# A fused attention and two-expert kernel on one core: attention output normalised in PSUM, low halves on either engine, a planner that keeps VectorE and GpSimd apart, and another order of tasks

## The chip, the cores and the metric

The kernel runs on one core of one Trainium2 chip. The metric is the device time of one execution in microseconds, the median of three runs. TensorE is the matrix engine (PE in the rows), VectorE is DVE, ScalarE is ACT, GpSimd is POOL, and SyncE (SP) issues the transfers.

## The reference

Attention with a bias that depends on the positions, then two expert layers on its output. Shapes: 4 batches, 8 heads, 576 positions, 64 elements a head; 2304 tokens of 512 elements; 2048 hidden elements.

```python
rel = (pos[:, None] - pos[None, :])
x = (np.log1p(np.abs(rel)) / np.log1p(np.maximum(pos[:, None], 1.0)))[..., None]
bias = np.maximum(x @ w1 + b1, 0.0) @ w2
scores = scale * np.matmul(q, k.transpose(0, 1, 3, 2)) + bias.transpose(2, 0, 1)[None]
attn = np.exp(scores - np.max(scores, axis=-1, keepdims=True))
attn = attn / (np.sum(attn, axis=-1, keepdims=True) + 1e-09)
x = np.matmul(attn, v)                       # to (2304, 512)
h = x @ w_in1; r = np.maximum(h, 0.0)
x = (s * (r * r) + b) @ w_out1               # first expert layer
h = x @ w_in2
out = (h - np.tanh(h)) @ w_out2              # second expert layer
```

## The kernel before

Every matmul operand is split into two half-precision parts, a high half (the value rounded) and a low half (what the rounding left), and products of halves are summed. So most values pass through a cast and a subtraction on their way.

**Attention.** The work is 144 units, each one pair of heads or half-rows by up to 128 query rows, and 36 groups of four units. A unit passes through these tasks: `qk` (12 matmuls on TensorE into `sp`, line 1003); `ttr` (VectorE, line 1035: adds the bias and finds the row's extreme) and a small addition to it on VectorE (line 1039); `ex` (the exponential with the row sum, ScalarE, line 1045); `hi` (the cast to `hl`, ScalarE line 1057 or VectorE line 1055); `lo` (the subtraction in two pieces of 64 and 512 columns, GpSimd, line 1064); `tr` (a transposing transfer, line 1070, `et` from `hl`); `pv` (14 matmuls into `xp`, lines 1083 and 1089). After the four units of a group, `x_tasks` normalises: VectorE adds a constant to the row sums (line 1127), inverts them (1128), multiplies the accumulator `xp` by them into an SBUF buffer `xf` (1129), casts that to `xh` (1143) and subtracts (1144); ScalarE squares `xf` for a norm (1147); a transfer transposes `xh` into `xt`.

**First expert layer.** Nine blocks of 256 tokens, tags f0 to f8. A block is 192 hidden-layer matmuls (`ph`, line 1499), passed on by eight rounds of ReLU (1512) and square (1517) on ScalarE, a cast (VectorE, 1522) and a subtraction (GpSimd, 1526) into `hr`, and 192 output-layer matmuls (`po`, line 1568), evacuated by VectorE (1582) or ScalarE (1587). The `po` tile is one bank of PSUM, whose two halves are used in turn. Lines 1194, 1197 and 1200 are three VectorE steps that convert a weight from 64-bit numbers; 585 and 580 split values into halves; 1775 sums weights; 1842, 2009 and 2018 are float32 sums of the second layer.

**Second expert layer.** Products of 24 matmuls (lines 1964 and 2092) on sums of quarter matrices; its weights are converted and split during the end of the first layer.

**What sets the order.** All of this is a list of tasks with priorities, and a planner in the kernel's file, `Schedule.forward`, plays them through on paper: each task has a cost per engine it may run on, corrected by a table `COST` (transfers by `XFER`), a priority corrected by a table `SHIFT`, and for some an engine fixed by `ENGINE` or `ONLY`. Rings of a given number of places (`ring`) hold back a task until a buffer is free in the plan. Tasks are emitted in the planned order, and every engine then works through its own queue in that order. When VectorE and GpSimd overlap in the plan, the cost of both grows by fractions called `SHARE` and `SHARE_POOL`. `AHEAD` is how far transfers may be issued ahead.

## Time and profile before

| quantity | us |
|---|---|
| median of three runs | 1077.86 |
| lowest, highest | 1072.72, 1078.9 |
| the profiled execution | 1072.9 |
| its span, first to last instruction | 1071.1 |

The mean granted clock of TensorE was 0.951. Busy time over the span: TensorE 962.1 us (90%), VectorE 898.9 (84%), ScalarE 664.7 (62%), GpSimd 350.7 (33%). These are averages over stretches that differ, so the rows below are cut by time: attention and the preparation of the first layer's weights to 171 us, attention together with the first layer to 560 us (the last score matmuls end at 559 us), the rest of the first layer to 741 us, and the second layer to the end.

### The profile page before, as it was taken

The numbers are of one execution on the slowest core, as the hardware profiler recorded it, in microseconds if no ns is written. First come the engines' busy times: TensorE is split into PE (matmuls) and PEld (weight loads), VectorE is DVE, ScalarE is ACT, GpSimd is POOL, SyncE is SP. The second block draws the span as 40 slices with busy tenths as digits, with TensorE's granted clock in tenths as the row PEclk, the third lists the DMA queues.
The fourth block names the chain that finished last, engine by engine and source line by source line (L and its number), as shares of the span: only waits on it lengthen the run. The fifth ranks groups of instructions, "written<-read, shape, count | busy, mean of one in ns | idle before, by whom it ended". The sixth has DMA issues, their size and how long they took to land.

```text
span 1071.1 us, 32375 instructions
## 1 busy us (share of the span) xinstructions
PE 962.1 (90%) x13370; PEld 820.5 (77%) x13370; DVE 898.9 (84%) x1914; ACT 664.7 (62%) x1279; POOL 350.7 (33%) x371
## 2 busy tenths in 40 slices
PE   5565658999998899999999898987999999999998
PEld 2222236778787688787888787877999999999998
DVE  6899899767668777786773989889999999999876
ACT  6788879868766576777753575656645543344433
POOL 6034355646456376585762342300000000000000
PEclk9667669999999999999999999999999999999999
DMA  9969987999999999989996705310101100100001
GB/s 340 360 153 250 296 230 149 208 211 255 244 181 234 201 171 199 206 172 194 173 171 167 300 10 173 105 36 16 32 23 41 42 22 31 32 22 22 21 2 41
DMA packets 261444, 153.66 MB, mean 143 GB/s; under 512 B 197680, under 2 KB 229552, under 8 KB 261296
## 3 DMA queue, kind: packets, MB, share of 16 engines
q1 hardware_dynamic: 261296, 151.59, 58.8%
q8 instruction: 104, 1.70, 0.7%
q14 instruction: 44, 0.36, 0.1%
HBM read 84.03 MB, written 20.33 MB: 97 GB/s over the span
## 4 chain that ended last, share of the span: by engine, by line
PE 55%; DVE 21%; DMA 12%; ACT 4%; issue 4%; POOL 3%; SPq 1%; DVEq 0%; ACTq 0%; POOLq 0%
PE acc L2092 13%; PE ph L1499 9%; PE pa L1964 8%; PE po L1568 8%; DMA et<-hl 8%; PE pb L1964 6%; PE sp L1003 3%; DVE w1big L585 3%; DVE sp L1035 2%; PE po L2092 2%; PE xp L1083 2%; POOL hr L692 1%; ACT e L1045 1%; DMA w1big<-in_wout 1%; DMA bi<-btd 1%
## 5 line engine op out<-in xcount | busy, mean ns | idle before, releaser
L1064 POOL TENSOR_TENSOR hl<-e,hl 128x64 f16<-128x64 f32 (+1 forms) x288 | 231.9, 828 | 221.0 <-ACT hl L1057 93.6
L1568 PE MATMUL po<-hr,w1big 128*128 128x256 f16 x1728 | 205.8, 275 | 13.2 <-ACT x L1587 8.6
L1568 PEld LDWEIGHTS <-w1big 128*128 128x128 f16 x1728 | 166.7, 99 | 39.2 <-issue 18.8
L1499 PEld LDWEIGHTS <-w1big 128*128 128x128 f16 x1728 | 165.2, 98 | 26.7 <-issue 8.0
L1964 PEld LDWEIGHTS <-w2big 128*128 128x128 f16 x3024 | 174.1, 98 | 4.2 <-issue 4.2
L2092 PEld LDWEIGHTS <-w1big 128*128 128x128 f16 x3024 | 172.8, 98 | 2.1 <-issue 2.1
L1045 ACT ACTIVATE e<-sp,mx 128x576 f32<-128x576 f32 x144 | 105.7, 734 | 53.7 <-DVE mx L1039 39.2
L1526 POOL TENSOR_TENSOR hr<-r,hr 128x512 f16<-128x512 f32 x72 | 100.4, 1396 | 115.8 <-DVE hr L1522 104.6
L1035 DVE CUSTOM_DVE_ANT_0 sp<-sp,bi 128x576 f32<-128x576 f32 x144 | 109.6, 761 | 31.9 <-PE sp L1003 26.5
L1499 PE MATMUL ph<-xt_own,w1big 128*128 128x256 f16 x960 | 112.5, 273 | 1.0 <-ACT r L1512 0.6
L1003 PE MATMUL sp<-ks,qs 64*128 64x288 f16 (+1 forms) x960 | 82.8, 298 | 13.9 <-ACT e L1045 11.3
L1083 PEld LDWEIGHTS <-et 128*128 128x128 f16 (+1 forms) x1440 | 54.9, 103 | 49.8 <-DMA et<-hl 26.6
L1499 PE MATMUL ph<-w1big 128*128 128x256 f16 x768 | 89.7, 275 | 1.6 <-ACT r L1512 1.2
L1083 PE MATMUL xp<-vp,et 128*128 128x64 f16 (+1 forms) x1440 | 65.5, 198 | 23.5 <-DMA et<-hl 17.8
L1057 ACT ACTIVATE hl<-e 128x576 f16<-128x576 f32 x100 | 67.5, 680 | 24.4 <-DMA et<-hl 21.1
L2092 PE MATMUL acc<-hr,w1big 128*128 128x128 f16 x1296 | 80.2, 219 | 1.8 <-DVE hr L585 1.2
L1003 PEld LDWEIGHTS <-qs 64*128 64x128 f16 (+1 forms) x960 | 46.3, 99 | 43.0 <-issue 32.8
L2092 PE MATMUL acc<-w2big,w1big 128*128 128x128 f16 x1296 | 79.1, 219 | 0.0
L1964 PE MATMUL pa<-w1big,w2big 128*128 128x128 f16 x960 | 61.2, 221 | 4.0 <-ACT w1big L1983 4.0
L1512 ACT ACTIVATE r<-ph 128x512 f32<-128x512 f32 x72 | 42.6, 592 | 31.0 <-PE ph L1499 22.4
L1522 DVE CAST hr<-r 128x512 f16<-128x512 f32 x72 | 42.2, 588 | 17.6 <-ACT r L1517 16.0
L1517 ACT ACTIVATE r<-r,sq 128x512 f32<-128x512 f32 x72 | 51.8, 720 | 1.5
(225 smaller groups left out, 1686.1 us busy)
## 6 DMA issues: line engine op xcount, KB each, us to landing
bi<-btd SPq DMA_DIRECT2D x64, 288.0 KB, 4.1
w1big<-in_wout SPq DMA_DIRECT2D x12, 1024.0 KB, 5.8
btd<-et SPq DMA_DIRECT2D x36, 295.5 KB, 4.4
w1big<-in_win SPq DMA_DIRECT2D x8, 1024.0 KB, 8.0
w2big<-in_win SPq DMA_DIRECT2D x8, 1024.0 KB, 12.8
x2d<-x SPq DMA_DIRECT2D x36, 128.0 KB, 2.2
w1big<-x2d SPq DMA_DIRECT2D x36, 128.0 KB, 2.4
outT<-xt_own SPq DMA_DIRECT2D x18, 256.0 KB, 2.2
```

Of the source, the lines that this page charges most:

```text
L1003: nc.tensor.matmul(out=out, lhsT=qs.tile[64 * h:64 * h + 64, sq, p * r:p * r + r], rhs=ks.tile[64 * h:64 * h + 64, sk, half * HS:(half + 1 ...
L1035: nc.vector.tensor_tensor_reduce(out=st, in0=st, in1=bi.tile.rearrange("p (a b) -> p a b", a=2), scale=-1.0 / KAP, scalar=3.0e38, op0=ALU. ...
L1045: nc.scalar.activation(out=put(e, row_tile("e")).rearrange("p (a b) -> p a b", a=2), in_=sp.tile[:, :, 0:HS], func=AF.Exp, scale=-1.0, bia ...
L1057: nc.scalar.activation(out=h[:, 0:S], in_=e.tile, func=AF.Copy)
L1064: (nc.gpsimd if eng == POOL else nc.vector).tensor_tensor(out=hl.tile[:, o:o + m], in0=e.tile[:, c:c + m], in1=hl.tile[:, c:c + m], op=ALU ...
L1083: nc.tensor.matmul(out=xp[r0:r0 + r, o:o + 64], lhsT=et.tile[:, n, r0:r0 + r], rhs=vp.tile[:, 0, n % 5, 64 * h:64 * h + 64], start=n == 0, ...
L1499: nc.tensor.matmul(out=ph.tile[:, fi, :], lhsT=win_ap(1, sw, m, f), rhs=xa(sx, m), start=m == 0 and j == 0, stop=m == KM - 1 and j == 2,)
L1517: nc.scalar.activation(out=r.tile, in_=r.tile, func=AF.Square, scale=sq[:, fp // 4:fp // 4 + 1])
L1526: (nc.gpsimd if e == POOL else nc.vector).tensor_tensor(out=rh[:, :, 1, :], in0=r.tile, in1=rh[:, :, 0, :], op=ALU.subtract)
L1568: nc.tensor.matmul(out=po.tile[:, :NB1], lhsT=wout_ap(1, sw, f, c), rhs=rhl[f // 8][:, f % 8, sr, :], start=f == 0 and j == 0, stop=f == K ...
L1964: nc.tensor.matmul(out=bank.tile[:, f * HT:(f + 1) * HT], lhsT=w[:, sw, m, f * 128:(f + 1) * 128], rhs=xs[:, sx, m], start=p in (1, 2, 5) ...
L2092: nc.tensor.matmul(out=bank.tile[:, o + c * HT:o + (c + 1) * HT], lhsT=w[:, sw, f, c * 128:(c + 1) * 128], rhs=g[:, sx, f], start=new and ...
```

## The change

- `x_tasks`: the buffer `xf` goes. `xp` becomes one tile of one bank, two halves used in turn, with a ring of 2. Scaling works in place in PSUM; cast (VectorE or ScalarE), subtraction (VectorE) and square (ScalarE) read PSUM; the constant and the inversion become tasks of their own, the constant on VectorE or GpSimd.
- The ring of `po` has 2 places in place of 1.
- The small addition behind `ttr`, both pieces of `lo` and the first layer's subtraction may run on VectorE or GpSimd; the first layer's cast on VectorE or ScalarE.
- The planner no longer stretches overlapping work: a VectorE task that uses the shared port (its `share` above 0) starts in the plan only when GpSimd's task is over, less 0.14 us, and the other way round. All tables are new, `AHEAD` is 8.71 for 5.97, a hold of SP's queue behind a late transfer is added.
- A block's hidden-layer matmuls are no longer chained behind the output-layer matmuls of the block before (`last = list(t_in1)`).

In the built program that gives these counts:

| task | before | after |
|---|---|---|
| first layer's subtraction | GpSimd 72 | GpSimd 34, VectorE 38 |
| first layer's cast | VectorE 72 | VectorE 12, ScalarE 60 |
| pieces of `lo` | GpSimd 288 | GpSimd 185, VectorE 103 |
| `hi` of a unit | VectorE 44, ScalarE 100 | VectorE 71, ScalarE 73 |
| addition behind `ttr` | VectorE 144 | VectorE 87, GpSimd 57 |
| cast of a group's output | VectorE 36 | VectorE 16, ScalarE 20 |
| `ph` and `po` matmuls ahead of unit 24's scores | 72, 0 | 12, 0 |
| `ph` and `po` matmuls ahead of unit 36's scores | 192, 188 | 192, 176 |
| `ph` and `po` matmuls ahead of the last scores | 1152, 1172 | 1248, 1184 |

Matmuls into `xp` that wait for VectorE or ScalarE on the same bank: 33 before, all for line 1129; 47 after, for accesses to the other half of the bank (27 line 1201, 8 line 1198, 5 line 1184, 4 line 1194, 3 line 1192). Matmuls into `po` that wait for an evacuation of the other half: 26 before, 27 after; 15 evacuations on ScalarE after the change also wait for matmuls into the other half.

```diff
@@ tables
-AHEAD = 5.97
+AHEAD = 8.71
-ONLY = {"I.fn": "dve", "I.sub": "dve", "J.fn": "dve", "J.c22": "dve", "I.add": "dve", "X.xsum": "dve", "P.wsum": "dve", "u.lo": "pool", "f.lo": "pool"}
+ONLY = {"I.fn": "dve", "I.sub": "dve", "J.fn": "dve", "J.c22": "dve", "I.add": "dve", "X.xsum": "dve", "P.wsum": "dve"}
 ENGINE = {
...
+    "f3.hi": "dve", "u0.mx_add": "dve", "f1.lo": "pool", "u2.mx_add": "dve", "u6.mx_add": "dve", "f8.lo": "dve",
+    "u12.mx_add": "dve", "f8.hi": "act", "f1.out": "act", "u16.lo_a": "pool", "u1.lo_a": "pool", "x6.eps":
...
@@ class Schedule, forward
-    SHARE, SHARE_POOL, SHARE_MAX = 0.65, 0.18, 2.1
+    BACK, BACK_MIN, BACK_HOLD = 0.5, 1.6, 1.1
+    LEAD, LONG = 0.14, 1.6
+    SHARE = 1.0
+                    if eng == "dve" and t.share > 0.0:
+                        at = max(at, port["pool"] - self.LEAD)
+                    elif eng == "pool" and t.opts[eng] < self.LONG:
+                        at = max(at, port["dve"] - self.LEAD)
-                if eng == "dve" and t.share > 0.0:
-                    rest = port["pool"] - at
-                    if rest > 0.0:
-                        cost = min(cost + t.share * rest, cost * self.SHARE_MAX)
-                        late("pool", self.SHARE_POOL * min(rest, cost))
-                    port["dve"], user["dve"] = at + cost, t
...
+                if eng == "pool" and cost < self.LONG or eng == "dve" and t.share > 0.0:
+                    port[eng] = at + cost
@@ rings
-("x", 1), ("h", 2), ("o", 1), ("r", 2), ("xt", 4), ("x2", 2), ("xf", 2), ("xh", 2), ("sum", 4),
+("x", 2), ("h", 2), ("o", 2), ("r", 2), ("xt", 4), ("x2", 2), ("xh", 2), ("sum", 4),
+    xp_all = ps_x.tile([128, 2, 256], F32, name="xp")
@@ units
-        t_lo = sc.add({POOL: 1.5, DVE: 0.7}, lo, [t_hi], d + 4, [], [e, hl])
+        t_lo = [
+            sc.add({POOL: 0.31, DVE: 0.15}, lo_a, [t_hi], d + 4, [], [e, hl]),
+            sc.add({POOL: 1.16, DVE: 0.69}, lo_b, [t_hi], d + 4, [], [e, hl]),
+        ]
-                put(xp_i, ps_x.tile([128, 512], F32, tag="xp", name="xp"))
+                put(xp_i, xp_all[:, xp_n(), :])
@@ x_tasks
+            x = xp_of[n].tile.rearrange("p (h d) -> p h d", d=64)
             nc.vector.tensor_tensor(
-                out=put(xf, x_p.tile([128, 256], F32, tag="xf", name="xf", bufs=2)).rearrange(
...
+                out=x, in0=x, in1=sum_of[n].tile.unsqueeze(2).to_broadcast([128, NP, 64]), op=ALU.mult,
...
+            if eng == DVE:
+                nc.vector.tensor_copy(out=xh.tile[:, 0:256], in_=xp_of[n].tile)
+            else:
+                nc.scalar.activation(out=xh.tile[:, 0:256], in_=xp_of[n].tile, func=AF.Copy)
...
+            nc.vector.tensor_tensor(out=xh.tile[:, 256:512], in0=xp_of[n].tile, in1=xh.tile[:, 0:256], op=ALU.subtract)
...
-                out=xf.tile, in_=xf.tile, func=AF.Square, accum_out=nrm[:, n:n + 1]
+                out=xp_of[n].tile, in_=xp_of[n].tile, func=AF.Square, accum_out=nrm[:, n:n + 1]
@@ first expert layer
-        last = t_poq.get(n - 1, [])[-1:]
+        last = list(t_in1)
-            def hi(_, rh=rh, r=r):
-                nc.vector.tensor_copy(out=rh[:, :, 0, :], in_=r.tile)
+            def hi(e, rh=rh, r=r):
+                if e == DVE:
+                    nc.vector.tensor_copy(out=rh[:, :, 0, :], in_=r.tile)
+                else:
+                    nc.scalar.activation(out=rh[:, :, 0, :], in_=r.tile, func=AF.Copy)
```

VectorE behind the last score tile, before: casts of the first layer (line 1522, `hr` from `r`) and the three conversion steps of the second layer's weights (`w2big`).

```order
L1522 CAST hr<-r 128x2x256 x4
L1194 TENSOR_SCALAR w2big<-w2big 128x1024
L1197 SCALAR_TENSOR_TENSOR w2big<-w2big 128x1024
L1522 CAST hr<-r 128x2x256
L1200 SCALAR_TENSOR_TENSOR w2big<-w2big 128x1024
```

The same place after: the subtraction (line 1584, which reads `r` and the high half in `hr`) stands where the cast stood.

```order
L1584 TENSOR_TENSOR hr<-r,hr 128x2x256 x3
L1248 TENSOR_SCALAR w2big<-w2big 128x1024
L1251 SCALAR_TENSOR_TENSOR w2big<-w2big 128x1024
L1584 TENSOR_TENSOR hr<-r,hr 128x2x256
L1254 SCALAR_TENSOR_TENSOR w2big<-w2big 128x1024
```

In each order 24 such instructions of the first layer stand behind the last score tile on VectorE: 24 casts before, 24 subtractions after.

ScalarE at that place, before: pairs of ReLU (line 1512, from `ph`) and square (1517).

```order
L1512 ACTIVATE r<-ph 128x512
L1517 ACTIVATE r<-r,sq_8369 128x512
L1512 ACTIVATE r<-ph 128x512
L1517 ACTIVATE r<-r,sq_8369 128x512
L1723 ACTIVATE junk,ss_w_137<-w2big 128x512 x2
```

After: the cast (line 1580) is the third of each round.

```order
L1567 ACTIVATE r<-ph 128x512
L1572 ACTIVATE r<-r,sq_8455 128x512
L1580 ACTIVATE hr<-r 128x2x256
L1567 ACTIVATE r<-ph 128x512
L1572 ACTIVATE r<-r,sq_8455 128x512
L1580 ACTIVATE hr<-r 128x2x256
L1781 ACTIVATE junk,ss_w_138<-w2big 128x512 x2
```

So 24 casts came to ScalarE's queue here, each between a square and the next ReLU.

TensorE at the first matmuls of the last group's attention output, before (in brackets the semaphore that the instruction waits for): score matmuls, then `xp`, which waits for VectorE's scaling of the group before.

```order
L1003 LDWEIGHTS qs
L1003 MATMUL sp<-ks,qs 128x288
L1083 LDWEIGHTS et [waits DMAHW4_49]
L1083 MATMUL xp<-vp,et 128x64 [waits DVE_49]
L1083 LDWEIGHTS et
L1083 MATMUL xp<-vp,et 128x64
```

After: output-layer matmuls, then `xp` (line 1131), which waits for ScalarE's square of the group before.

```order
L1626 LDWEIGHTS w1big
L1626 MATMUL po<-hr,w1big 128x256
L1131 LDWEIGHTS et [waits DMAHW6_49]
L1131 MATMUL xp<-vp,et 128x64 [waits Activation_49]
L1131 LDWEIGHTS et
L1131 MATMUL xp<-vp,et 128x64
```

The group before lies in the other half of the bank; the wait moved from VectorE's first step to ScalarE's last one.

## Rows read from the trace of the kernel before

**Rows 1.** Busy time by stretch: us, then busy and instructions per engine, granted clock, DMA share.

```profile
...
30.00:171.00 141.00, 88.25 (x755) 42.84 (x751) 133.50 (x259) 115.79 (x225) 47.14 (x45) 0.71 0.90 248
171.00:217.00 46.00, 42.23 (x630) 30.68 (x627) 39.86 (x89) 40.42 (x85) 31.79 (x34) 1.00 0.85 173
217.00:560.00 343.00, 328.55 (x4385) 272.18 (x4382) 252.22 (x685) 238.32 (x532) 207.82 (x254) 0.99 1.01 202
560.00:600.00 40.00, 39.02 (x470) 34.23 (x469) 19.92 (x41) 17.14 (x34) 14.03 (x11) 1.00 0.77 235
600.00:741.00 141.00, 122.41 (x1177) 107.50 (x1175) 129.37 (x194) 85.83 (x152) 29.72 (x17) 0.96 0.26 88
741.00:1040.00 299.00, 298.66 (x5339) 298.54 (x5337) 283.49 (x577) 139.10 (x208) 0.00 (x0) 1.00 0.09 27
...
```

**Rows 2.** Waits from 217 to 560 us: engine, line, releaser: total us, times, longest.

```profile
...
PEld L1083 <- DMA et<-hl: 9.8, 15, 1.6
...
PE xp L1083 <- DMA et<-hl: 5.9, 10, 1.0
...
PE sp L1003 <- ACT e L1045: 2.5, 3, 1.4
...
PE po L1568 <- ACT x L1587: 2.1, 3, 1.0
...
```

**Rows 3.** Timeline from 589 us: start, us, engine, line, operation.

```profile
...
588.75 7.37 PE L1499 MATMUL ph<-w1big 128*128 128x256 f16 x66
...
590.21 0.41 DVE L1522 CAST hr<-r 128x512 f16<-128x512 f32 x1
...
590.76 2.01 POOL L1526 TENSOR_TENSOR hr<-r,hr 128x512 f16<-128x512 f32 x1 [1.56 <-DVE hr L1522]
590.98 0.60 ACT L1512 ACTIVATE r<-ph 128x512 f32<-128x512 f32 x1 [1.27 <-PE ph L1499]
...
591.68 1.64 DVE L1194 TENSOR_SCALAR w2big<-w2big 128x1024 uint32<-128x1024 uint32 x1
...
```

**Rows 4.** VectorE groups by form, 560 to 741 us: busy us, mean ns, idle before.

```profile
...
L1522 DVE CAST hr<-r 128x512 f16<-128x512 f32 x24 | 13.7, 570 | 8.5 <-ACT r L1517 7.4 <-issue 1.1
L1197 DVE SCALAR_TENSOR_TENSOR w2big<-w2big 128x1024 uint32<-128x1024 uint32 x8 | 11.4, 1439 | 0.1
...
L1194 DVE TENSOR_SCALAR w2big<-w2big 128x1024 uint32<-128x1024 uint32 x8 | 8.2, 1042 | 0.0
L1197 DVE SCALAR_TENSOR_TENSOR w2big<-w1big,w2big 128x1024 uint32<-128x1024 uint32 x4 | 4.9, 1215 | 0.0
...
L1842 DVE TENSOR_TENSOR w1big<-w1big 128x256 f32<-128x256 f32 x8 | 4.1, 536 | 0.0
L1200 DVE SCALAR_TENSOR_TENSOR w2big<-xt_own,w2big 128x512 uint32<-128x512 uint32 x4 | 3.7, 920 | 0.0
...
L1194 DVE TENSOR_SCALAR w2big<-w1big 128x1024 uint32<-128x1024 uint32 x4 | 2.9, 726 | 0.9 <-DMA w1big<-in_wout 0.9
...
L1200 DVE SCALAR_TENSOR_TENSOR w2big<-w2big 128x512 uint32<-128x512 uint32 x4 | 2.7, 678 | 0.0
...
```

**Rows 5.** GpSimd groups by form, the whole span.

```profile
...
L1064 POOL TENSOR_TENSOR hl<-e,hl 128x512 f16<-128x512 f32 x144 | 178.2, 1238 | 0.0
...
```

**Rows 6.** VectorE groups by form, 741 to 1040 us, where GpSimd is idle.

```profile
...
L2009 DVE TENSOR_TENSOR w1big<-w1big 128x512 f32<-128x512 f32 x30 | 20.5, 684 | 4.2 <-ACT w1big L2000 4.1
...
L1842 DVE TENSOR_TENSOR w1big<-w1big 128x256 f32<-128x256 f32 x28 | 11.1, 414 | 0.0
...
```

**Rows 7.** VectorE groups by form, 217 to 560 us.

```profile
...
L1129 DVE TENSOR_TENSOR xf<-xp,sum 128x256 f32<-128x256 f32 x26 | 11.0, 425 | 8.7 <-PE xp L1089 6.9
...
```

**Rows 8.** Waits from 560 to 741 us.

```profile
...
PE po L1568 <- ACT x L1587: 6.5, 7, 1.1
...
```

**Rows 9.** VectorE groups by form, 30 to 171 us.

```profile
...
L1200 DVE SCALAR_TENSOR_TENSOR w1big<-w1big 128x1024 uint32<-128x1024 uint32 x14 | 20.9, 1500 | 0.1
...
L1197 DVE SCALAR_TENSOR_TENSOR w1big<-w1big 128x1024 uint32<-128x1024 uint32 x14 | 18.0, 1295 | 0.1
...
```

More of the change, by code (lines that the diff above doesn't have):

```diff
@@ L271, in forward @@
         pool = {}
[L272 to L283 removed]
+        port = dict(dve=0.0, pool=0.0)
         def enter(t):
@@ L342, in forward @@
             if isinstance(cost, tuple):
-                free[eng] = at + cost[0]
+                hold = cost[0]
+                if eng == "sp" and hold > self.BACK_HOLD and bus - at > self.BACK_MIN:
+                    hold += self.BACK * (bus - at - self.BACK_MIN)
+                free[eng] = at + hold
                 bus = max(bus, at + self.DMA_START) + cost[1]
@@ L2097, in out_product @@
         t = sc.add(
-            {PE: 1.345}, mm, t_gl[k, p] + t_wp[1, s, p] + last_pe, base, [bank] if new else [], [bank],
+            {PE: 1.345}, mm, t_gl[k, p] + t_wp[1, s, p] + last_pe, base, [bank] + more if new else [], [bank] + more,
         )
@@ L2114, in psum_add @@
                     out=out(), in0=half(bank.tile, h), scalar=osc, in1=add(), op0=ALU.mult, op1=ALU.add
-                ), [t] + deps, pr, takes, list(uses) + [bank], share=0.0,
+                ), [t] + deps, pr, takes, list(uses) + [bank] + more, share=0.0,
             )
```

155 lines of the change are left out of this document (81 added, 74 removed), and 238 rows, old and new, of tables (ENGINE, SHIFT).

## The prediction

> **What bounds the kernel now.** I read first the table of busy time by stretch [rows 1], because the share of the whole run hides that the limit changes hands. The reader is to see, in each row, which engine is busy for nearly the whole stretch. From 30 to 171 us that is VectorE (133.5 of 141 us), while TensorE has 88.25 us of work at a granted clock of 0.71. From 171 to 560 us it is TensorE: 42.23 of 46 us and 328.55 of 343 us, so 3.8 and 14.4 us are idle. From 560 to 600 us TensorE again (39.02 of 40). From 600 to 741 us VectorE, with 129.37 of 141 us, while TensorE has 18.6 us idle. From 741 to 1040 us TensorE works 298.66 of 299 us; nothing that is edited lies there, and I leave it as it is. So a gain must come out of one of four places: VectorE's time in the first and the third stretch, or TensorE's 18 idle us in the second.
>
> Second I read what TensorE waits for in the long second stretch [rows 2]. The largest waits are on landings of the transposed probabilities (9.8 and 5.9 us), then on the exponentials (2.5) and on evacuations (2.1). Third I asked what VectorE pays for GpSimd. In the timeline [rows 3] a TENSOR_SCALAR of line 1194 takes 1.64 us while a GpSimd subtraction of line 1526 runs, and that subtraction takes 2.01 us; without such company the first has a group mean of 0.726 us [rows 4], and GpSimd's subtraction of the same width has a mean of 1.238 us over 144 instructions, many of which have company too [rows 5]. Both engines pay for running together.
>
> **Third stretch, 560 to 741 us.** The change gives the low halves of the last three blocks to VectorE and their high halves to ScalarE, and leaves GpSimd empty there. The order of instructions shows it: 24 casts go away from VectorE behind the last score tile, and 24 subtractions come.
> - Contention that ends. By groups against the same form without company [rows 4]: casts 24 x (0.570 − 0.41 [rows 3]) = 3.8 us; line 1194 8 x (1.042 − 0.726) = 2.5; line 1197 8 x (1.439 − 1.215) = 1.8; the half-width conversions, of which three groups of four are long and three are short, 12 x (0.920 − 0.678) = 2.9; line 1842 8 x (0.536 − 0.414 [rows 6]) = 1.0. Sum 12.0 us.
> - Casts gone: 24 x 0.41 = 9.8 us.
> - Subtractions come: no such operation of that size ran on VectorE before. The nearest row is the subtraction-like TENSOR_TENSOR of 512 float32 elements without GpSimd, 0.684 us [rows 6], so 24 x 0.684 = 16.4 us. If the half-precision operand made it as cheap as the cast it would be 9.8; if it cost what two operations of 256 at 0.414 cost, 19.9.
>
> Net −12.0 − 9.8 + 16.4 = −5.4 us, between −12 and −1.9. ScalarE takes 24 casts; the nearest price is its own pass over 512 elements in this stretch, 0.60 us [rows 3], so 14 us on top of 17 + 86 us in the 181 of these two rows [rows 1]: it stays off the path.
>
> **Second stretch, 171 to 560 us.** In the order of TensorE 1152 hidden-layer and 1172 output-layer matmuls of the first expert layer stand ahead of the last score matmuls; afterwards it is 1248 and 1184. That is 108 more. One costs 7.37 / 66 = 0.112 us [rows 3], so 12.1 us of TensorE work comes forward out of the third stretch, whose end VectorE sets. In itself it gains nothing, since the stretch that receives it is bound by TensorE. It gains where it fills the 14.4 idle us. These are waits on transposes and exponentials, that is, on the chain through ScalarE, GpSimd and the DMA queue, and independent matmuls placed there do cover them if they are placed rightly. I take half of 12.1, −6 us; the ends are −12 and 0.
>
> Against that stand new waits. The attention output is now scaled, rounded, subtracted and squared where the matmuls left it, and the two halves of its tile lie in one bank. In the built program 47 of its matmuls wait for an access by VectorE or ScalarE to the other half, 27 of them for the square, the last of the four steps; before, 33 waited, all for the one scaling of 0.425 us [rows 7], after which the bank was free. Ahead of 23 of the 47 stands less than 1.0 us of other matmuls since the access, against 6 of 33 (estimated from the matmul counts and the length of one). So 17 more may be felt. The row nearest to a felt one is the output layer's wait for its evacuation, 6.5 us over 7 times, 0.93 each [rows 8]: up to 17 x 0.93 = 16 us. The lower end is below nothing: the second place in the ring lets the planner issue the next group's matmuls before the last step is over, which cannot beat the 14.4 idle us. I take +3, since the accesses of most groups are short (0.4 us) and the planner's order puts on average 1.5 us of matmuls behind them. Net −3 us, between −12 and +16.
>
> The low halves and casts that VectorE takes over in the second half of this stretch (42 us of work ahead of the last score tile) I cost at nothing: VectorE has 343 − 252 = 91 us free there, and GpSimd sheds as much. Without that cover they would stand ahead of the score tiles and cost TensorE the same.
>
> **First stretch, to 171 us.** Here exclusion in the planner could give back what the conversions pay: line 1200 takes 1.500 us and line 1197 1.295 us, 14 times each [rows 9], against 1.215 without company: 14 x 0.285 + 14 x 0.08 = 5.1 us; with the smaller groups some 6.5. The work put ahead of each score tile is the same within 4 us from unit 12 to unit 36. But 60 fewer hidden-layer matmuls stand ahead of unit 24's scores (12 for 72), 60 x 0.112 = 6.7 us, which return before unit 36, where TensorE has 3.8 us idle. So 2.9 us come back as a loss. −6.5 + 3 = −3.5 us, between −8 and +7.
>
> **Sum.** −3.5 − 3 − 5.4 = −12 us. The profiled execution took 1072.9 us (span 1071.1 and 1.8 around it), so 1061 us. The median of the three runs is 1077.86, 1.0046 times that execution, and on its scale the forecast is **1066 us**. About 1% (10.8 us) is what a measurement of this kernel can tell from no change.
>
> **Rivals.**
> *The bank decides (slower).* The halves are not two buffers: whoever works on one keeps the others off the bank. Then all 17 newly exposed waits cost 0.93 us, 16 us, and besides, 15 evacuations on ScalarE that now wait for matmuls in the other half hold back what is queued behind them, above all exponentials, each for up to the 12 matmuls of 0.112 us: 20 us at most, half of it taken, 10. With the other terms (−3.5 − 5.4) that is +17, so 1090, 1095 us on the median's scale. It turns into a loss from the point where the waits cost more than 9 us. For it: the waits are in the built program. Against it: before, 26 such waits of the output layer stood in the program, and TensorE lost only 2.1 us behind ScalarE's evacuations in the long stretch [rows 2]. By the Trainium skill, "PSUM — Partial Sum Buffer", section "PSUM bank collisions raise a hardware error", accesses of different engines have to be kept apart by bank and quadrant of partitions and not by address. The waits of the built program agree; what they cost no run here shows yet.
>
> *No change.* The idle time of TensorE in the second stretch is of another kind: the transposes land when they land, the matmuls that were moved only push the next scores back, and the third stretch ends on TensorE's order, since the whole path from hidden layer to output layer still passes through three engines. Then the 12.1 us come forward into a full stretch (+6), and the third gives back 5.4: 1073, or 1078 us. For it: the chain's waits are on landings [rows 2]. Against: VectorE is busy for 92% from 600 to 741 us.
>
> *Exclusion is worth more than the durations show.* If a GpSimd instruction holds VectorE for its whole length, so that part of the stall lies between VectorE's instructions and not in them, GpSimd's departure frees 24 x 1.238 = 29.7 us in the third stretch and not 12.0. Then the sum is −12 − 17.7 = −30, so 1043, or 1048 us. For it: 1.64 for 0.726 us in the timeline [rows 3]. Against: VectorE's gaps in the third stretch are small, 11.6 us of the 141. By the Trainium skill, "SBUF — State Buffer", section "Who interferes with whom", the port pair that VectorE shares with GpSimd is an exclusive lock and the second comer is blocked fully. The trace agrees in part: the 1.64 us are far above 0.726, but the GpSimd instruction beside it is longer as well (2.01 against 1.238), which a plain lock on one side would not give.
>
> **Chances.** Forecast 0.45 (of it 0.30 faster by over 1%, 0.13 within, 0.02 slower); the bank 0.20 (0.16 slower, 0.04 within); no change 0.20 (0.14 within, 0.04 slower, 0.02 faster); exclusion 0.15 (all faster). That is 0.47 faster, 0.31 within 1%, 0.22 slower. The range leaves out the outer half of the exclusion case and the worse half of the bank's: 1042 to 1092 us.
>
> **What the next profile would show.** In the third stretch no GpSimd, the subtractions on VectorE near 0.68 us, line 1194's counterpart near 0.73, and VectorE's stretch shorter by about 5 us; if the subtractions come out at 0.9 or the stretch is bound by ScalarE, that step is wrong. In the second, TensorE busy for more than 97% with the attention output's matmuls waiting for ScalarE's square or VectorE's subtraction in short pieces of 3 us together; 15 us or more there is the rival of the bank. In the first, conversions at 1.25 us and the last score matmuls of unit 24 no later than 171 us. The prediction is wrong if the last score matmuls end later than 565 us, since nothing behind them can make up for that, or if the fixed part behind 741 us changes its length.

## The result, and the profile after

The changed kernel took 1065.21 us in the median of 8 runs (1062.53 to 1070.37), the kernel before 1077.21 us beside it (1072.72 to 1078.9): a ratio of 0.9903, with a 95% interval of 0.9875 to 0.9931. That is 10.4 us less by the ratio, and 12.0 us between the two medians. The forecast was 1066 us and 12 us less. The sum came out; its composition did not, as the experiments show. The profiled execution took 1063.98 us, its span is 1062.2 us, the granted clock 0.955.

Busy time of the changed kernel in the same stretches as [rows 1] (us, then busy time and instructions of TensorE, weight loads, VectorE, ScalarE and GpSimd, granted clock, DMA share, GB/s):

```profile
...
30.00:171.00 141.00, 91.06 (x934) 45.82 (x932) 133.58 (x267) 126.58 (x256) 59.89 (x64) 0.75 0.95 265
171.00:217.00 46.00, 44.56 (x556) 33.68 (x549) 33.14 (x96) 32.19 (x72) 16.72 (x25) 0.96 0.84 176
217.00:560.00 343.00, 325.82 (x4286) 272.07 (x4286) 242.80 (x670) 229.33 (x531) 151.16 (x204) 0.99 0.97 194
560.00:600.00 40.00, 36.95 (x478) 31.09 (x472) 24.85 (x53) 21.05 (x48) 0.48 (x1) 0.96 0.74 218
600.00:741.00 141.00, 124.78 (x1297) 112.61 (x1297) 126.30 (x200) 100.44 (x184) 0.00 (x0) 0.98 0.28 93
741.00:1040.00 299.00, 299.00 (x5347) 298.89 (x5345) 274.36 (x556) 152.38 (x231) 0.00 (x0) 1.00 0.09 29
...
```

From 30 to 171 us VectorE is as full as before. GpSimd has one instruction of 0.48 us behind 560 us and none behind 600. ScalarE has 18.5 us more from 560 to 741 us, of which the 24 casts are 14.9 (0.628 us each); TensorE has 2.4 us more from 600 to 741 us because the second layer starts earlier (its first output matmuls, L2149, at 731.3 us, L2092 of the kernel before at 739.8). Behind 741 us TensorE is full, as before.

The third stretch's VectorE groups from 563 to 732 us, by form (instructions, then busy us and mean ns):

```profile
...
L1584 DVE TENSOR_TENSOR hr<-r,hr 128x512 f16<-128x512 f32 x24 | 16.3, 685 | 6.7 <-ACT hr L1580 6.7
...
L1251 DVE SCALAR_TENSOR_TENSOR w2big<-w2big 128x1024 uint32<-128x1024 uint32 x8 | 9.7, 1214 | 0.0
L1248 DVE TENSOR_SCALAR w2big<-w2big 128x1024 uint32<-128x1024 uint32 x8 | 5.5, 684 | 1.5 <-DMA w2big<-in_win 1.5
...
L1254 DVE SCALAR_TENSOR_TENSOR w2big<-xt_own,w2big 128x512 uint32<-128x512 uint32 x4 | 2.8, 688 | 0.0
...
L1248 DVE TENSOR_SCALAR w2big<-xt_own 128x512 uint32<-128x512 uint32 x4 | 1.7, 422 | 0.0
L1248 DVE TENSOR_SCALAR w2big<-w2big 128x512 uint32<-128x512 uint32 x4 | 1.7, 420 | 0.0
L1900 DVE TENSOR_TENSOR w1big<-w1big 128x256 f32<-128x256 f32 x4 | 1.6, 417 | 0.0
...
```

Here the durations of the prediction can be read off one by one against [rows 4]. The 24 subtractions take 0.685 us (0.684 was taken from [rows 6]). Line 1248, which was 1194, takes 0.684 for 1.042; line 1251, which was 1197, 1.214 for 1.439; the half-width form of line 1254 0.688 for 0.920; line 1900, which was 1842, 0.417 for 0.536. So the company of GpSimd cost what these groups said; in the half-width forms of line 1248 it cost more than the sum had, which is taken up below.

What TensorE waits for from 217 to 560 us, against [rows 2]:

```profile
...
PE po L1626 <- DVE x L1640: 4.0, 3, 2.9
...
PEld L1131 <- DMA et<-hl: 3.6, 5, 1.4
...
PE po L1626 <- ACT x L1645: 2.5, 5, 0.9
...
PE xp L1131 <- DMA et<-hl: 2.1, 3, 1.3
...
PE xp L1131 <- ACT xh L1194: 1.6, 1, 1.6
...
PE xp L1131 <- ACT xp L1201: 1.5, 3, 0.9
...
```

The attention output's matmuls wait 1.6 + 1.5 us for ScalarE's cast and square in the bank, in four waits, the 3 us that were put down for it, and 2.1 + 3.6 us for transposes, where it was 15.7. Over the whole span, the first stretch included, there are nine such waits of 9.3 us, seven of them for ScalarE:

```profile
...
PE xp L1131 <- ACT xp L1201: 5.8, 5, 2.8
...
PE xp L1131 <- ACT xh L1194: 2.1, 2, 1.6
...
```

The chain that ended last, pieces between 540 and 760 us (start, us, what):

```profile
...
579.35 12.31 PE ph L1554 x96
...
618.52 18.36 PE ph L1554 x168
...
663.77 18.34 PE ph L1554 x168
...
702.92 0.98 PE po L1626 x8
...
711.98 2.66 DVE w1big L622 x2
...
732.12 1.33 DVE hr L622 x2
...
737.18 0.66 DVE hr L622
...
```

Until 703 us the third stretch's chain runs over TensorE's hidden and output layers, with ScalarE's evacuations between them, and then over VectorE's preparation of weights until 738. The prediction had one engine setting this end; here one follows the other.

### The profile page after: what moved, and what is told of

It is laid out like the page before. It is cut to its first block, busy times and chain, and to the rows that moved or that the text cites. A ratio compares the mean times of both kernels' runs of the same rounds, so it can differ in the third digit from the quotient of the medians.

```text
span 1062.2 us, 32293 instructions
## 1 busy us (share of the span) xinstructions
PE 957.4 (90%) x13370; PEld 821.9 (77%) x13370; DVE 869.7 (82%) x1902; ACT 687.5 (65%) x1357; POOL 249.5 (23%) x305
## 4 chain that ended last, share of the span: by engine, by line
PE 70%; DVE 10%; ACT 9%; DMA 6%; issue 4%; SPq 1%; POOL 0%; DVEq 0%; ACTq 0%; POOLq 0%
PE po L1626 16%; PE ph L1554 14%; PE acc L2149 13%; PE pa L2019 8%; PE pb L2019 6%; PE sp L1040 4%; PE xp L1131 3%; PE po L2149 2%; DMA et<-hl 2%; PE pb L760 2%; ACT e L1086 2%; DVE sp L1072 1%; PE xp L1137 1%; ACT x L1645 1%; DMA w1big<-in_win 1%
## 5 line engine op out<-in xcount | busy, mean ns | idle before, releaser
L1626 PE MATMUL po<-hr,w1big 128*128 128x256 f16 x1728 | 203.3, 274 | 14.6 <-ACT x L1645 10.6
L1103 POOL TENSOR_TENSOR hl<-e,hl 128x512 f16<-128x512 f32 (+1 forms) x185 | 158.8, 871 | 191.5 <-ACT hl L1098 76.9
L2149 PEld LDWEIGHTS <-w1big 128*128 128x128 f16 x3024 | 172.7, 98 | 0.0
L1072 DVE CUSTOM_DVE_ANT_0 sp<-sp,bi 128x576 f32<-128x576 f32 x144 | 107.0, 775 | 34.9 <-PE sp L1040 30.1
L1554 PE MATMUL ph<-xt_own,w1big 128*128 128x256 f16 x960 | 115.1, 276 | 3.8 <-ACT r L1567 3.3
L2149 PE MATMUL acc<-hr,w1big 128*128 128x128 f16 x1296 | 79.7, 219 | 0.0
L2149 PE MATMUL acc<-w2big,w1big 128*128 128x128 f16 x1296 | 79.2, 219 | 0.0
L1103 DVE TENSOR_TENSOR hl<-e,hl 128x512 f16<-128x512 f32 (+1 forms) x103 | 52.8, 526 | 12.3 <-ACT hl L1098 7.0
L1096 DVE CAST hl<-e 128x576 f16<-128x576 f32 x71 | 38.5, 543 | 24.5 <-ACT e L1086 17.4
L1645 ACT ACTIVATE x<-po,bcol,esc 128x128 f32<-128x128 f32 (+1 forms) x69 | 26.7, 443 | 48.6 <-PE po L1626 46.3
L1098 ACT ACTIVATE hl<-e 128x576 f16<-128x576 f32 x73 | 48.9, 679 | 7.3 <-DMA et<-hl 6.9
## 6 DMA issues: line engine op xcount, KB each, us to landing
w1big<-in_win SPq DMA_DIRECT2D x8, 1024.0 KB, 10.7
```

Source lines behind the costliest of these rows:

```text
L1072: nc.vector.tensor_tensor_reduce(out=st, in0=st, in1=bi.tile.rearrange("p (a b) -> p a b", a=2), scale=-1.0 / KAP, scalar=3.0e38, op0=ALU. ...
L1096: nc.vector.tensor_copy(out=h[:, 0:S], in_=e.tile)
L1098: nc.scalar.activation(out=h[:, 0:S], in_=e.tile, func=AF.Copy)
L1103: eng_of(eng).tensor_tensor(out=hl.tile[:, o:o + m], in0=e.tile[:, c:c + m], in1=hl.tile[:, c:c + m], op=ALU.subtract)
L1554: nc.tensor.matmul(out=ph.tile[:, fi, :], lhsT=win_ap(1, sw, m, f), rhs=xa(sx, m), start=m == 0 and j == 0, stop=m == KM - 1 and j == 2,)
L1626: nc.tensor.matmul(out=po.tile[:, :NB1], lhsT=wout_ap(1, sw, f, c), rhs=rhl[f // 8][:, f % 8, sr, :], start=f == 0 and j == 0, stop=f == K ...
```

## The experiments

Each run gives two kinds of numbers. The ratio to the kernel before is from timed executions on one chip. Inside each profiled execution I read three times: the start of unit 36's bias addition on VectorE (line 1035, later 1072), that of the last unit, and the end of the span. They cut the run into a first part, a second part ("36 to last") and the rest.

| run | ratio, 95% interval | unit 36 | last unit | 36 to last | last to end |
|---|---|---|---|---|---|
| before | 1 | 219.4 | 559.5 | 340.1 | 511.6 |
| changed | 0.9903 (0.9875 to 0.9931) | 208.0 | 563.0 | 355.0 | 499.2 |
| changed, again | 0.9888 (0.9861 to 0.9915) | 210.6 | 569.9 | 359.3 | 498.5 |
| e1_lo_back | 0.9987 (0.9970 to 1.0003) | 209.4 | 564.0 | 354.6 | 508.0 |
| e3_no_lo | 0.9920 (0.9898 to 0.9941) | 210.0 | 567.5 | 357.5 | 499.1 |
| e4_fewer_ph | 0.9870 (0.9848 to 0.9892) | 209.1 | 568.7 | 359.6 | 495.2 |
| e5_out_in_sbuf | 0.9904 (0.9882 to 0.9925) | 208.6 | 566.3 | 357.7 | 499.6 |
| b1_lo_on_vector | 0.9940 (0.9917 to 0.9963) | 222.2 | 567.0 | 344.8 | 506.0 |
| b2_fewer_ph | 0.9983 (0.9965 to 1.0000) | 221.4 | 566.1 | 344.7 | 510.8 |
| b3_both | 0.9918 (0.9895 to 0.9940) | 219.8 | 562.5 | 342.7 | 504.1 |
| e10_f6_held | 0.9998 (0.9980 to 1.0016) | 210.6 | 566.3 | 355.7 | 505.8 |
| a7_more_gpsimd | 1.0068 (1.0041 to 1.0094) | 226.3 | 583.1 | 356.8 | 499.4 |
| b4_exclusion_plan | 1.0178 (1.0144 to 1.0212) | 212.5 | 568.4 | 355.9 | 527.2 |
| a12_short_transposes | 0.9801 (0.9764 to 0.9838) | 210.4 | 558.6 | 348.2 | 500.1 |

The part "36 to last" scatters by 5 us between executions of the same plan (354.6 to 359.6 in the five with the changed plan and no edit ahead of the last unit). The part "last to end" of the changed plan lies within 1.1 us in the four executions where it was not edited (498.5 to 499.6: changed, changed again, e5 and a7).

Three theories stood at the start. *VectorE sets the third stretch*, and the gain there comes from the engines that were swapped in f6 to f8. *TensorE sets it*, and the gain comes from the matmuls that were moved ahead. *The bank* takes back part of it in the second stretch.

**The swap undone (e1_lo_back).** Swap is used here for the exchange of f6 to f8: the cast from VectorE to ScalarE, the subtraction from GpSimd to VectorE. Only the engine on which the instructions are issued is changed, not the plan:

```diff
             def hi(e, rh=rh, r=r):
+                e = DVE if n >= 6 else e
             def lo(e, rh=rh, r=r):
+                e = POOL if n >= 6 else e
```

> The changed kernel with the same plan, but in the blocks f6 to f8 the subtraction goes back to GpSimd and the cast back to VectorE. If VectorE sets the end of the third stretch (theory), contention returns (+12.0 us), 16.4 us of subtractions leave VectorE and 9.8 us of casts come back: about 5 us slower than the changed kernel, near 1070 us. If TensorE sets it (rival), and the stretch was shortened only by the matmuls that went ahead of it: within 2 us of 1065.

Measured: 0.9987, nearly all of the gain gone, and 8.8 us more behind the last unit. Groups of this run from 564 to 745 us:

```profile
...
L1586 POOL TENSOR_TENSOR hr<-r,hr 128x512 f16<-128x512 f32 x24 | 39.8, 1661 | 89.1 <-DVE hr L1579 65.2 <-DVE esc L1612 23.4 <-DVE na L1513 0.4
...
L1579 DVE CAST hr<-r 128x512 f16<-128x512 f32 x24 | 13.7, 578 | 5.5 <-ACT r L1572 4.2 <-POOL hr L1586 1.0 <-issue 0.3
...
L1251 DVE SCALAR_TENSOR_TENSOR w2big<-w2big 128x1024 uint32<-128x1024 uint32 x8 | 10.6, 1321 | 0.1
...
L1248 DVE TENSOR_SCALAR w2big<-w2big 128x1024 uint32<-128x1024 uint32 x8 | 6.4, 802 | 2.2 <-DMA w2big<-in_win 2.2
...
```

The contention is back: 1.661 us for GpSimd's subtraction, 0.578 for the cast, 0.802 and 1.321 for lines 1248 and 1251, which were 0.684 and 1.214. VectorE is busy for 445.1 us behind the last unit, for 435.6 in the changed kernel. And TensorE waits for GpSimd's subtractions, which it did nowhere in the changed kernel's third stretch (in the kernel before 2.7 us, in two waits):

```profile
...
PE po L1628 <- POOL hr L1586: 4.3, 4, 1.9
...
```

The swap matters, by more than the 5.4 us of the sum: 8.8 us behind the last unit, where VectorE has 9.5 us more to do.

**The subtractions left out (e3_no_lo).**

```diff
             def lo(e, rh=rh, r=r):
+                if n >= 6:
+                    return
```

> The changed kernel without the subtractions of the blocks f6 to f8 (their low halves are left out, so the output is not the reference's). If VectorE sets the end of the third stretch: 10 to 16 us less, 1049 to 1055 us. If TensorE does: 0 to 3 us less.

Measured: 499.1 us behind the last unit, 0.1 less than with them. 16.4 us of VectorE work are gone and nothing comes of it, where 10 to 16 us were expected if VectorE set the end. So in the changed kernel VectorE alone does not set the third stretch.

**Fewer matmuls there (e4_fewer_ph).**

```diff
+                    pr = ((0, 0), (0, 1), (1, 0))[:2 if n >= 7 else 3]
-                        for j, (sw, sx) in enumerate(((0, 0), (0, 1), (1, 0))):
+                        for j, (sw, sx) in enumerate(pr):
```

> The changed kernel without the third product (low half of the weight) of the hidden layer in the blocks f7 and f8: 128 matmuls less, 128 x 0.112 = 14.3 us of TensorE work, nearly all of it behind the last score tile. If TensorE sets the end of the third stretch: 12 to 14 us less, 1051 to 1053 us. If VectorE does: 0 to 4 us less.

Measured: 4.0 us less behind the last unit for 14.3 us of TensorE work. So TensorE alone does not set it either. Both theories in their plain form fall. One reading of the two runs is that TensorE ends this stretch with VectorE some 4 us behind it; that the two hand over to each other, as the chain above has it, is another, and the runs do not tell them apart.

**The attention output in SBUF (e5_out_in_sbuf).** The plan stays; the scaling writes the buffer of the kernel before, and the other three steps read it:

```diff
+            xf_of[n] = x_p.tile([128, 256], F32, tag="xf", name="xf", bufs=2)
...
-                nc.vector.tensor_copy(out=xh.tile[:, 0:256], in_=xp_of[n].tile)
+                nc.vector.tensor_copy(out=xh.tile[:, 0:256], in_=xf_of[n])
...
-                out=xp_of[n].tile, in_=xp_of[n].tile, func=AF.Square, accum_out=nrm[:, n:n + 1]
+                out=xf_of[n], in_=xf_of[n], func=AF.Square, accum_out=nrm[:, n:n + 1]
```

> The changed kernel with the same plan, but the scaled attention output goes to a buffer in SBUF as before, and cast, subtraction and square read it there, so that the bank is held by the scaling alone. If the waits across the halves of the bank cost the 3 us of the prediction: about 3 us less, near 1062. If they cost more (the rival of the bank): 8 us less or more. If all of them are covered, or the change to SBUF operands costs VectorE as much: within 1.5 us of 1065.

Measured: 0.9904 for 0.9903. TensorE's waits from 217 to 560 us in this run:

```profile
...
PEld L1131 <- DMA et<-hl: 6.2, 10, 1.3
...
PE xp L1131 <- DMA et<-hl: 4.0, 7, 1.2
...
PE po L1628 <- ACT x L1647: 3.2, 5, 1.0
...
PE po L1628 <- DVE x L1642: 3.1, 3, 1.6
...
```

No row of the attention output's matmuls names the cast or the square any more; those waits are gone (over the whole span 0.3 us are left of the 9.3), and the waits for transposes are longer instead (6.2 + 4.0 for 3.6 + 2.1 us). The time is the same within the intervals, some 3 us: the 16 us of the rival fall, and 3 us would hardly be seen. The edit also makes VectorE's cast and subtraction slower (the last section has the rows, 4.6 us in all from 217 to 560 us), so that a small gain could be hidden by that; against it VectorE's busy time from unit 36 to the last is only 1.0 us longer (253.63 for 252.66).

**The swap alone, in the kernel before (b1_lo_on_vector), fewer matmuls (b2_fewer_ph), and both (b3_both).** The edits are those above, the other way round and in the plan before. The changed kernel ran again beside them, as b0_after_again:

> The changed kernel once more, to stand beside the three others: 1065 us, ratio 0.990.

It gave 0.9888. The edit of b1:

```diff
             def lo(e, rh=rh, r=r):
+                e = DVE if n >= 6 else e
...
+                if n >= 6:
+                    nc.scalar.activation(out=rh[:, :, 0, :], in_=r.tile, func=AF.Copy)
```

> The kernel before with the same plan, but in the blocks f6 to f8 the subtraction on VectorE and the cast on ScalarE, as the change has it. If VectorE alone ends the third stretch of the kernel before (theory): the 8.7 us by which undoing this made that stretch longer come off, near 1069 us. If TensorE stands close behind VectorE there, since the 12 us of matmuls have not been moved out (rival): 0 to 4 us less, 1073 to 1077.

> The kernel before without the third product of the hidden layer in f7 and f8, 128 matmuls or 14.3 us of TensorE work less behind the last score tile. If VectorE alone ends that stretch: 0 to 4 us less, 1073 to 1077. If TensorE does: 12 us less or more.

> Both edits in the kernel before. If the two engines stand close to each other in the third stretch, so that it takes both to shorten it: 10 to 14 us less, 1064 to 1068, clearly more than the two single gains added. If one engine alone ends it: no more than the larger of the single gains.

Measured behind the last unit: 5.6 us less for the swap, 0.8 for the matmuls, 7.5 for both; whole times by the ratios 6.5, 1.8 and 8.8 us less. In the kernel before, VectorE and GpSimd were the limit of that stretch and TensorE was not: the swap takes 8.3 us of busy time off VectorE behind the last unit (454.3 to 446.0), and 5.6 come out as time. The two gains add, with 1.1 us over, which is the scatter. Neither branch of two expectations was met: 5.6 lies between 8.7 and the 0 to 4 of b1, and 7.5 is neither the 10 to 14 of b3 nor the larger single gain. Groups of b1 from 560 to 742 us:

```profile
...
L1530 DVE TENSOR_TENSOR hr<-r,hr 128x512 f16<-128x512 f32 x24 | 16.6, 690 | 11.9 <-ACT hr L1523 11.7
...
L1523 ACT ACTIVATE hr<-r 128x512 f16<-128x512 f32 x24 | 15.0, 625 | 0.5
...
L1197 DVE SCALAR_TENSOR_TENSOR w2big<-w2big 128x1024 uint32<-128x1024 uint32 x8 | 9.6, 1220 | 0.1
...
L1194 DVE TENSOR_SCALAR w2big<-w2big 128x1024 uint32<-128x1024 uint32 x8 | 5.3, 686 | 0.5 <-DMA w2big<-in_win 0.5
...
```

The same durations as in the changed kernel: 0.690 us for the subtraction, 0.686 for line 1194, 1.220 for line 1197. The swap by itself is worth 5.6 us in the kernel before, near the 5.4 us of the sum.

With e1 this makes a table of four, in us behind the last unit: neither the swap nor the rest of the change 511.6, the rest alone 508.0 (e1), the swap alone 506.0 (b1), both 499.2. The rest of the change is worth 3.6 us without the swap and 6.8 with it; the swap 5.6 alone and 8.8 beside the rest. Each is worth 3.2 us more where the other is present; the scatter of such a figure is about 1 us.

**What stood ahead of the last scores (e10_f6_held).** Block f6's first half is held back at issue:

```diff
             if emit:
-                t.fn(eng)
+                nqk -= t.key.endswith(".qk")
+                if nqk and t.key.startswith("f6."):
+                    held.append((t, eng))
+                else:
+                    t.fn(eng)
+                if not nqk:
+                    for x, y in held:
+                        x.fn(y)
+                    held = []
```

> The changed kernel with the same plan, but everything of block f6 that stands ahead of the last score matmuls (96 hidden-layer matmuls, 10.7 us of TensorE, and the ReLU, squares, casts and subtractions that follow them) is issued right behind those. If matmuls put into the second stretch cost their full length there (measured so far: 14.2 us later for 127 more) and the third gives back only about 7 of the 10.7: the last score tile 10 us earlier and the whole 3 to 5 us faster, near 1061. If they fill idle time of TensorE, as the prediction had it by half: last score tile 5 us earlier, the whole 3 to 8 us slower.

By then I held the view that the moved matmuls cost their full length, because the part "36 to last" is 14.2 us longer over the means (357.3 of six executions against 343.1 of four) with 128 more matmuls in it in the profiles (4463 for 4335). This view fell. Without the 96 the part takes 355.7 us, 1.6 less than that mean and inside its scatter of 5 us, and the part behind the last unit 6.6 us more; the whole loses 10 to 12 us by the ratios (0.9998 against 0.9903 and 0.9888; the profiled execution was among the three fastest of its twelve, within 0.3 us of the fastest, and shows less). Neither branch of the expectation had this: the last unit hardly moves, and the whole is slower by more than 3 to 8 us. Second part, and the 40 us behind the last unit, of this run:

```profile
...
210.60:566.30 355.70, 331.68 (x4382) 274.56 (x4383) 249.61 (x701) 231.52 (x539) 154.52 (x209) 0.98 0.98 195
566.30:606.30 40.00, 37.97 (x456) 32.97 (x455) 17.51 (x40) 20.69 (x43) 0.68 (x1) 1.00 0.51 157
...
```

and of the changed kernel:

```profile
...
208.00:563.00 355.00, 337.82 (x4463) 281.75 (x4464) 252.66 (x701) 233.88 (x543) 154.19 (x209) 0.99 0.97 195
563.00:603.00 40.00, 36.54 (x425) 30.88 (x424) 24.96 (x48) 22.76 (x51) 0.48 (x1) 0.96 0.74 238
...
```

In the second part TensorE has 24.0 us idle without the matmuls (355.7 − 331.68) and 17.2 with them (355 − 337.82): they go mostly into idle time. In the 40 us behind it VectorE is busy for 24.96 us with them and 17.51 without, 7.4 us more, about what the stretch is shorter by. f6's first ReLU starts at 526.8 us in the changed kernel, at 566.8 with the block held and at 577.2 in the kernel before. Its first subtraction on VectorE starts 12.7 us behind the last unit, at 575.7 us, and 20.9 us behind it with the block held; the first conversion of `w2big`, which stands behind five such subtractions in VectorE's order, 24.7 and 32.2 us behind it. So this work can be done where VectorE otherwise stands idle.

**GpSimd given more to do (a7_more_gpsimd).**

```diff
+    def dummy():
+        nc.gpsimd.tensor_tensor(out=scr16, in0=ones32, in1=ones32, op=ALU.subtract)
...
+            f = lambda _, g=g: (dummy(), dummy(), g(_))
```

> The changed kernel with the same plan, but two subtractions of 128 columns on GpSimd, on data that nobody needs, are issued with each of the 48 conversion steps of the first layer's weights (96 in all, half of them before the first unit). If VectorE's contention sets the first stretch: VectorE's excess over uncontended durations up to unit 36 rises by 4 to 8 us and unit 36's bias comes as much later; the whole 3 to 8 us slower, 1069 to 1073. If the stretch was shortened by something else (an earlier start, another order): excess up, unit 36 within 2 us, the whole within 3 us of 1065.

Measured: 1.0068, 18 to 19 us slower than the changed kernel; unit 36 comes 17 us later. GpSimd's groups up to 226 us:

```profile
...
L1271 POOL TENSOR_TENSOR scr<-ones 128x128 f16<-128x128 f32 x96 | 71.1, 740 | 6.4
L1103 POOL TENSOR_TENSOR hl<-e,hl 128x512 f16<-128x512 f32 x30 | 40.7, 1360 | 20.7 <-ACT hl L1098 14.0 <-DVE hl L1096 6.6
...
```

The 96 subtractions take 0.740 us each, 71 us in all; the ten that met no VectorE instruction took 0.39 to 0.40 us. VectorE's excess (each instruction's duration less the median of its form without GpSimd beside it, summed up to unit 36) is 18.4 us for 11.6. These 6.8 us are what was expected; the other 10 are idle time of VectorE, 6 of them ahead of the first unit, where the added work stands in GpSimd's queue ahead of the bias. So a delay of the first part does reach the end, and contention is part of it, but this run does not size that part by itself.

**Exclusion in the plan alone (b4_exclusion_plan).** The four lines of the planner in the kernel before, with its own tables, and `share=1.0` for the conversions.

> The kernel before with its own tables, but the planner keeps VectorE and GpSimd apart as the change does (and counts the conversions as users of the port). If the exclusion in the plan is what lowers the contention: VectorE's excess up to unit 36 falls from 23 us to 12 or less and unit 36 comes 5 to 11 us earlier. If it needs the tables that were made for it: excess down by less than 5 us, unit 36 not earlier, the whole slower than 1078.

Measured: 1.0178. VectorE's excess up to unit 36 is 23.0 us, as it was (23.3). Unit 36 comes 6.9 us earlier only because the plan put 14 us less VectorE work ahead of it, and the part behind the last unit is 15.6 us longer. The rule of the planner by itself lowers no contention here. Whether in the changed kernel the new tables do it, or the engines chosen, was not tried alone.

**Shorter transposes (a12_short_transposes).**

```diff
+            if u < 36:
+                nc.sync.dma_start_transpose(out=x, in_=hl.tile)
+            else:
+                nc.sync.dma_start_transpose(out=x[:, 0:5], in_=hl.tile[:, 0:640])
```

> The changed kernel with the same plan, but from unit 36 on the transposing transfer carries only the first 640 of its 1152 columns, and the matmuls of the attention output use the five blocks that it brings in place of nine (their number stays; most of the low half is left out). If transfers set the pace from 217 to 563 us (mean busy share of the DMA engines 0.97 there, 1.01 in the kernel before), which would be why neither 11 us of lead at unit 36 nor 96 matmuls less move the last score tile by as much: the last score tile 10 to 18 us earlier, where TensorE's own work stops it, and the whole 8 to 18 us faster, 1047 to 1057. If TensorE or the chain through ScalarE and VectorE sets the pace: last score tile within 4 us of 563 to 570, the whole within 4 us of 1065.

Measured: 0.9801, 9 to 11 us less than the changed kernel (0.9903 and 0.9888); most of the low half in `hl` is left out here. The part "36 to last" takes 348.2 us, 9.1 less than the mean of the plan. That part in this run, and then in the kernel before:

```profile
...
210.40:558.60 348.20, 335.50 (x4463) 280.17 (x4464) 250.24 (x700) 233.41 (x543) 154.10 (x209) 1.00 0.79 159
...
```

```profile
...
219.40:559.50 340.10, 325.65 (x4335) 269.80 (x4334) 249.49 (x676) 237.61 (x530) 205.96 (x252) 0.99 1.02 203
...
```

With a DMA share of 0.79 TensorE has 12.7 us idle in it, and 337.8 of 355 us busy became 335.5 of 348.2. In the kernel before the share is 1.02. So transfers hold up the second part by some 9 us in the changed kernel, fewer than the 10 to 18 expected, and TensorE's work stands close behind. Whether it is the load of the DMA engines or the time that one transpose takes to land, this run does not tell apart, since it shortens both.

## Why the prediction was right, and where its steps were not

**Third stretch, forecast −5.4 us.** The mechanism holds, and most of its prices: contention ends, the subtraction costs 0.685 us, and the swap alone gives 5.6 us behind the last unit in the plan before (b1). That this meets the 5.4 is in part luck, because one term was too small. The half-width conversions were all priced at 0.678 us without company, but those of line 1194 are shorter: 0.420 and 0.422 us as line 1248 of the changed kernel, above. In the kernel before, from 560 to 741 us, they were

```profile
...
L1194 DVE TENSOR_SCALAR w2big<-xt_own 128x512 uint32<-128x512 uint32 x4 | 3.6, 895 | 0.0
...
L1194 DVE TENSOR_SCALAR w2big<-w2big 128x512 uint32<-128x512 uint32 x4 | 2.6, 656 | 0.0
...
```

so that both of these groups were long. With them the half-width forms lose 4.7 us and not 2.9, and line 1194's full width 2.9 and not 2.5; the contention that ends is some 14 us and not 12.0, and VectorE's net some 7.6. VectorE's busy time behind the last unit shows 8.3 us (b1) and 9.5 (e1). In the changed plan nearly all of it comes out as time (8.8 us, e1), in the plan before two thirds (5.6 us, b1). What failed is the sentence that VectorE sets this end, so that matmuls taken out of the stretch "in themselves" gain nothing. The stretch is 12.4 us shorter, not 5.4, and holding back what was moved costs 6.6 of that (e10). 5.6 and 6.6 make 12.2 of the 12.4, but in this order alone: taken the other way round the parts are 3.6 and 8.8.

**Second stretch, forecast −3 us.** That matmuls fill TensorE's idle time was right, and perhaps mis-sized: half of their length was to be absorbed, and 1.6 us of 10.7 came out as time, with a scatter of 5 us. What was wrong is where the gain shows. By e10 it is not TensorE's time in this stretch that was won but the earlier start of f6's chain on ScalarE and VectorE. The 3 us for the bank stand in the rows, and e5 shows no time that they cost. The rival built on them, with the Trainium skill's rule on banks ("PSUM — Partial Sum Buffer", section "PSUM bank collisions raise a hardware error") beside it, was right that such waits come, and wrong in number and price: 17 of 0.93 us were to be felt, and there were four of 3.1 us together from 217 to 560 us. Where they are taken away, waits for transposes are as much longer.

**First stretch, forecast −3.5 us.** Conversions got cheaper as forecast. The rows of the changed kernel from 30 to 171 us, against [rows 9]:

```profile
...
L1254 DVE SCALAR_TENSOR_TENSOR w1big<-w1big 128x1024 uint32<-128x1024 uint32 x14 | 18.0, 1287 | 0.1
L1251 DVE SCALAR_TENSOR_TENSOR w1big<-w1big 128x1024 uint32<-128x1024 uint32 x14 | 17.1, 1218 | 0.1
...
```

14 x (1.500 − 1.287) + 14 x (1.295 − 1.218) = 4.1 us for 5.1. But unit 36 came 11.4 us earlier, not 3.5 (209.3 us over the six executions, 220.7 over four of the plan before), and then the second part took 14.2 us longer. At the last unit the changed kernel is 3.5 us behind, 2.8 over the means. The sign of the attention's whole share was wrong: forecast −6.5 for both stretches together, measured +3.5.

**The sum.** −3.5 − 3 − 5.4 = −12 was forecast; +3.5 up to the last unit and −12.4 behind it, −8.9 us in the profiled executions, were measured, and −10.4 by the ratio of the runs. Two errors of opposite sign met; that the forecast came out so near is luck. The sign by which the prediction would have been known to be wrong, last score matmuls later than 565 us, was wrong too: in the second profile of the changed kernel the last score matmul ends at 569.2 us, and the runs beside it still gain 1.1%.

**The rivals.** No change and the bank are out. Exclusion worth more than the durations is out in the form in which it was put, 23 us from the third stretch: b1 gives 5.6. The Trainium skill's exclusive lock ("SBUF — State Buffer", section "Who interferes with whom") is not needed beyond what the durations show, because the stall lies in them. The prediction saw the trace agree with that lock in part, since GpSimd's subtraction was longer too (2.01 us). It left out what ran before. The kernel before, a subtraction without company and the VectorE step ahead of the one in [rows 3]:

```profile
...
582.39 1.16 POOL L1526 TENSOR_TENSOR hr<-r,hr 128x512 f16<-128x512 f32 x1 [2.05 <-DVE hr L1522]
...
590.54 1.21 DVE L1200 SCALAR_TENSOR_TENSOR w2big<-w2big 128x1024 uint32<-128x1024 uint32 x1
...
```

Line 1200's step runs for its usual 1.21 us, to 591.75. GpSimd's subtraction starts in it at 590.76, 0.99 us before its end, and takes 2.01 us, 0.85 more than the 1.16 alone. Line 1194's step starts in that one and ends 0.55 us after it, for 0.684 alone. So whoever came first kept its time, and the next one waited for all but 0.13 to 0.14 us of it, VectorE and GpSimd alike. The trace agrees with the lock in full here.

**What stays open.** Why the second part of the changed plan takes 14 us longer than that of the plan before. It is not the moved matmuls (1.6 us, e10) and not the bank (e5). Shorter transposes take 9 us off that part (a12), but the transfers are as many in both plans (share times length: 1.02 x 340.1 = 347 us before, 0.97 x 355.0 = 344 after). The 42 us of low halves and casts that VectorE took over there, costed at nothing, and the waits of the exponentials for GpSimd's addition (25.5 us over 15 times in the changed kernel's waits) were not tried by themselves. Nor is it shown which edit brought unit 36 forward; VectorE's busy time up to there fell by 13.7 us (195.1 to 181.4) and its excess by 11.7 (23.3 to 11.6), but e5 has 14.7 and unit 36 at the same time. The second place of the `po` ring, the longer `AHEAD`, the hold of SP's queue and the hidden layers no longer chained were not tried alone either.

## What to carry to other kernels

Where two engines take turns in a stretch, ask of each what happens if its work is taken away: here neither 16 us less on VectorE nor 14 us less on TensorE moved the end by more than 4, and yet an earlier start of the chain that feeds both moved it by 6.6. Low-half subtractions beside a busy VectorE are better on VectorE itself, once the cast has an engine of its own (0.685 us against 1.66 on GpSimd, and its neighbours get 0.1 to 0.5 us back each). An event that comes earlier in the middle of a run says little until it is followed to the end: 11 us at unit 36 were gone at the last unit.

## What the runs showed of the hardware

A GpSimd subtraction of 128 float32 columns took 0.740 us on average beside a busy VectorE, more than half of the 1.360 us that one of 512 columns took in the same run (a7); without company they took 0.39 to 0.40 us there and 1.16 us in the kernel before. Beside a busy VectorE short pieces are no bargain, since each can wait for a VectorE instruction.

In the third stretch of the kernel before, the 24 GpSimd subtractions and the conversions beside them went one after the other in the order in which they came, as in the rows under the rivals, with one exception: at 629.43 us a subtraction took 3.47 us, while two VectorE steps and a cast ran through. Conversions of 1024 elements that started during a subtraction ended 0.55 us (line 1194) or 1.08 us (line 1197) behind it, casts of 512 elements 0.28 us, however long they had waited: their own length less some 0.13 us.

Rounding and subtracting 256 elements on VectorE is not slowed by GpSimd when the input lies in PSUM. VectorE's groups of the changed kernel from 217 to 560 us:

```profile
...
L1198 DVE TENSOR_TENSOR xh<-xp,xh 128x256 f16<-128x256 f32 x25 | 10.5, 420 | 3.1 <-ACT xh L1194 1.9 <-ACT e L1086 0.5 <-PE xp L1137 0.3
...
L1192 DVE CAST xh<-xp 128x256 f16<-128x256 f32 x10 | 4.2, 423 | 0.9 <-PE xp L1137 0.7
...
```

and of e5, where the same two steps read SBUF:

```profile
...
L1200 DVE TENSOR_TENSOR xh<-xf,xh 128x256 f16<-128x256 f32 x24 | 13.2, 548 | 2.5 <-ACT xh L1196 2.0 <-issue 0.3
...
L1194 DVE CAST xh<-xf 128x256 f16<-128x256 f32 x10 | 5.8, 578 | 0.3
...
```

0.420 and 0.423 us against 0.548 and 0.578, at the same work of GpSimd beside them. Over the whole trace, split by whether a GpSimd instruction ran at the same time, the subtraction from PSUM takes 0.420 us with one and 0.422 without, the cast 0.422 and 0.421. From SBUF (e5) the subtraction takes 0.642 and 0.420, the cast 0.732 and 0.291: alone, the cast from SBUF is the faster one.

The mean busy share of the DMA engines reaches 1.02 over 340 us in the kernel before. Shorter transposes took it from 0.97 to 0.79 in the changed kernel and gave 9 us; whether by the share or by the shorter landing stays open. The prediction's table of stretches [rows 1] has that column, and no term of the sum used it.
